# Q and K by Strassen's seven products on pairs of W tiles and token chunks

## The chip, the cores and the metric

One core of one Trainium2 chip. The time is that of one execution on the device in microseconds; a kernel's figure is the median of its runs. PE is the matrix engine, DVE, ACT and POOL are the vector, scalar and GpSimd engines, SP is the engine that issues most DMAs.

## The reference

A layer norm, an attention block of 32 heads and a Mish MLP on the same normalised input, joined by a gate (cut to what is computed; all fp32):

```python
B, S, D, H, F = 1, 2048, 1024, 32, 3584
xn = layernorm(x)                                    # no scale, no shift
q, k, v = split(xn @ wqkv)                           # wqkv: D x 3D, 32 heads of 32
p = softmax(q @ k.T * 32 ** -0.5)                    # per head
s = (p @ v) @ wo
h = xn @ w1 + b1
m = (h * tanh(softplus(h))) @ w2
out = x + s * silu(m)
```

## The kernel before

Every large product is made in three matmuls on numbers split into a high part, rounded to the format that PE takes at full pace, and a low part, the rest: high x high, high x low, low x high (THREE). ACT makes a high part by a copy, DVE or POOL the low part by a subtraction (`low`, L295). A matmul is 128 x 128 by 128 x 512.

The program has these stages, one behind the other on PE.

1. **V, two passes** (L473 to L559). The first pass takes x in 16 tiles of 128 tokens, normalises and transposes it into xc, four chunks of 512 tokens (chunk c has two tiles, xc[c][0] and xc[c][1], of four k slices each, high and low side by side), and makes V's first 512 columns from it. The second pass (L548) makes the other 512 columns. Each group v_group is 24 matmuls into one of 8 PSUM banks; ACT copies it out, SP stores it. Beside them w1_early (L449) loads tiles of w1, POOL splits them, and SP stores the split tiles to w1s for the MLP: 12 tiles (W1_V). x_store keeps chunks 1 to 3 in DRAM (xs).
2. **Q and K** (L682 to L713). 16 tiles of 128 columns (f even Q, odd K) times 4 chunks, 24 matmuls each (L688) into one of 8 banks. ACT copies the high part out, DVE makes the low part, ACT's queue stores both. qk_load and qk_split bring the next tile of W. Beside it presplit (L659) takes half tiles: the other 16 tiles of w1 and the first 16 row tiles of w2 (W2_Q), 64 jobs, each a load, a POOL cast, a POOL subtraction and a store. From f = 12 on, four score matmuls of head 0 (s_mm, L613) stand behind each group, with a row maximum each on DVE.
3. **Attention with the MLP** (L719 to L1273). PE's order comes from a planner, Plan: it keeps a clock for each engine and rings for buffers and banks, and at each step takes the instruction that is ready and has the least due time. Streams: t (scores transposed, exponentials on ACT), s (scores for the maxima of the next heads), h and y (first and second product of the MLP) and the narrow column matmuls pv (P times V) and zp. POOL adds up the exponentials z, 15 adds of 128 x 2048 a head (L874); seven p tiles hold exponentials (ring "p"). LEAN is a row of digits, one for each 21 us of the planner's PE clock, each choosing a set of small shifts of due times. Row tiles of w2 that were not split in stage 2 are split during the MLP's first chunk (w2_op, L963): SP loads half a tile, ACT makes the high part, POOL the low part (L987), SP stores it to w2s.
4. **Output projection** (op, L1215).

DMAs of SP and ACT go out in the order of their queues. Where an instruction waits, all behind it on the same engine wait too.

## Time and profile before

| what | value |
|---|---|
| median of 3 runs (lowest to highest) | 3391.5 us (3391.26 to 3392.14) |
| profiled execution, first to last instruction (span) | 3390.7 us |
| median of the runs less that span | 0.8 us |
| V, second pass, and Q and K | 110 to 201 us, 201 to 565 us |
| attention with MLP, output projection | 565 to 3212 us, 3212 to 3386 us |
| PE's granted clock, mean | 1.00 |

The page gives no time of the profiled execution beside its span. Rows of groups read: line, engine, operation, written tile <- read tiles, shapes, count, busy us, mean ns of one, idle time just before and what ended it. Rows of windows read: from and to in us, length, busy us (and count) of PE, of PE's weight loads, of DVE, ACT and POOL, the granted clock, the share of the DMA engines, GB/s. Rows of a timeline and of the chain begin with start and length in us. Rows of waits end with total us, times, longest us.

### The profile page before, as it was taken

The numbers are of one execution on the slowest core, as the hardware profiler recorded it, in microseconds if no ns is written. First come the engines' busy times: TensorE is split into PE (matmuls) and PEld (weight loads), VectorE is DVE, ScalarE is ACT, GpSimd is POOL, SyncE is SP. The second block draws the span as 40 slices with busy tenths as digits, with TensorE's granted clock in tenths as the row PEclk, the third lists the DMA queues.
The fourth block names the chain that finished last, engine by engine and source line by source line (L and its number), as shares of the span: only waits on it lengthen the run. The fifth ranks groups of instructions, "written<-read, shape, count | busy, mean of one in ns | idle before, by whom it ended". The sixth has DMA issues, their size and how long they took to land.

```text
span 3390.7 us, 45610 instructions
## 1 busy us (share of the span) xinstructions
PE 3375.7 (100%) x17059; PEld 2495.2 (74%) x17059; DVE 2350.2 (69%) x3765; ACT 1960.6 (58%) x3112; POOL 2432.7 (72%) x724
## 2 busy tenths in 40 slices
PE   8999999999999999999999999999999999999999
PEld 7888888677777777776777777777777767777787
DVE  6111136888887787887888778878888788886543
ACT  5211113666667767666666676666666666666621
POOL 1323334888899998888888888888888888888800
PEclk9999999999999999999999999999999999999999
DMA  6977878334344454343333544343445433333382
GB/s 204 303 263 266 286 262 265 106 113 125 100 131 135 137 172 150 104 121 107 119 113 113 168 131 120 105 128 106 122 116 189 118 118 113 113 119 119 131 308 83
DMA packets 284465, 517.02 MB, mean 152 GB/s; under 512 B 88186, under 2 KB 134266, under 8 KB 261498
## 3 DMA queue, kind: packets, MB, share of 16 engines
q1 hardware_dynamic: 264532, 472.42, 44.4%
q10 hardware_dynamic: 19712, 41.69, 3.3%
q8 instruction: 135, 2.21, 0.3%
q14 instruction: 86, 0.70, 0.1%
HBM read 374.31 MB, written 138.67 MB: 151 GB/s over the span
## 4 chain that ended last, share of the span: by engine, by line
PE 99%; DMA 0%; ACT 0%; DVE 0%; SPq 0%; issue 0%
PE y L1116 18%; PE h L1026 18%; PE t L845 14%; PE s L763 13%; PE pv L892 13%; PE qk L688 10%; PE v L357 5%; PE op L1215 5%; PE zp L918 1%; PE pt L426 0%; PE s L615 0%; DMA qstack<-mt 0%; DMA vraw<-in_A_wqkv_dram 0%; PE mtp L592 0%; ACT p L284 0%
## 5 line engine op out<-in xcount | busy, mean ns | idle before, releaser
L874 POOL TENSOR_TENSOR z<-z,p 128x2048 f32<-128x2048 f32 x448 | 2067.6, 4615 | 176.6 <-ACT p L284 149.2
L284 ACT ACTIVATE p<-t,zero 128x512 f32<-128x512 f32 x2048 | 1382.0, 689 | 601.8 <-PE t L845 588.9
L769 DVE TENSOR_REDUCE mx<-s 128x1 f32<-128x512 f32 x1984 | 1327.7, 686 | 402.2 <-PE s L763 398.1
L1116 PE MATMUL y<-w,act 128*128 128x512 f32 x2688 | 932.7, 390 | 0.1
L845 PE MATMUL t<-qstack,kstack 128*128 128x512 f32 x2048 | 798.2, 392 | 1.3 <-DMA qstack<-mt 1.3
L763 PE MATMUL s<-kstack,qstack 128*128 128x512 f32 x1984 | 774.8, 392 | 0.0
L1026 PE MATMUL h<-xr,w 128*128 128x512 f32 x2016 | 704.3, 390 | 0.0
L1116 PEld LDWEIGHTS y<-w,act 128*128 128x128 f32 x2688 | 503.6, 188 | 114.7 <-issue 5.9
L845 PEld LDWEIGHTS t<-qstack,kstack 128*128 128x128 f32 x2048 | 383.8, 188 | 109.4 <-issue 21.0
L892 PE MATMUL pv<-p,v 128*32 128x512 f32 x4096 | 459.3, 594 | 0.0
L763 PEld LDWEIGHTS s<-kstack,qstack 128*128 128x128 f32 x1984 | 370.9, 188 | 110.6 <-issue 18.4
L1026 PEld LDWEIGHTS h<-xr,w 128*128 128x128 f32 x2016 | 378.1, 188 | 83.4 <-issue 4.2
L688 PE MATMUL qk<-xc,qkw 128*128 128x512 f32 x1536 | 351.0, 389 | 0.0
L688 PEld LDWEIGHTS qk<-xc,qkw 128*128 128x128 f32 x1536 | 288.1, 188 | 59.8
L892 PEld LDWEIGHTS pv<-p,v 128*32 128x32 f32 x4096 | 123.4, 110 | 283.1 <-issue 282.0
L1138 DVE TENSOR_TENSOR yacc<-yacc,y 128x512 f32<-128x512 f32 x416 | 282.9, 681 | 44.1 <-PE y L1116 43.0
L874 POOL TENSOR_TENSOR z<-p,p 128x2048 f32<-128x2048 f32 x32 | 148.0, 4626 | 210.2 <-PE zp L918 108.7
L1026 PE MATMUL h<-xc,w 128*128 128x512 f32 x672 | 230.1, 391 | 0.1
L295 DVE TENSOR_TENSOR qst<-qk,qst 128x512 fp32r<-128x512 f32 x64 | 44.3, 692 | 258.1 <-ACT qst L287 250.3
L287 ACT ACTIVATE qst<-qk 128x512 fp32r<-128x512 f32 x64 | 38.3, 598 | 306.0 <-PE qk L688 280.0
L676 POOL CAST pw<-praw 128x512 fp32r<-128x512 f32 x64 | 40.1, 627 | 236.0 <-DMA w1s<-pw 124.5
L357 PE MATMUL v<-vw,xc 128*128 128x512 f32 x768 | 180.7, 394 | 0.0
(94 smaller groups left out, 2372.1 us busy)
## 6 DMA issues: line engine op xcount, KB each, us to landing
w<-w1s SPq DMA_DIRECT2D x112, 1024.0 KB, 5.1
w<-w2s SPq DMA_DIRECT2D x200, 512.0 KB, 4.8
qstack<-qs SPq DMA_DIRECT2D x96, 256.0 KB, 6.4
kstack<-ks SPq DMA_DIRECT2D x96, 256.0 KB, 5.9
praw<-in_B_w_dram SPq DMA_DIRECT2D x64, 256.0 KB, 4.9
qs<-qst ACTq DMA_DIRECT2D x32, 512.0 KB, 3.8
w1s<-pw SPq DMA_DIRECT2D x32, 512.0 KB, 5.0
ks<-qst ACTq DMA_DIRECT2D x32, 512.0 KB, 4.3
```

Of the source, the lines that this page charges most:

```text
L284: nc.scalar.activation(out_, in_, fn, bias=zero if bias is None else bias, scale=scale)
L357: nc.tensor.matmul(ps, xc[t // 4][k // HK][:, a, k % HK, (t % 4) * P:(t % 4 + 1) * P], vw[i, k // 2][:, b, k % 2], start=n == 0, stop=n == ...
L688: nc.tensor.matmul(ps, w[:, a, k], xc[c][k // HK][:, b, k % HK], start=n == 0, stop=n == 3 * KT - 1)
L763: nc.tensor.matmul(sp_, qst[h % 3][:, qt * P:(qt + 1) * P], kst[h % 3][:, kc * 512:(kc + 1) * 512], start=True, stop=True)
L769: nc.vector.reduce_max(tiles["mx"][:, qt, kc:kc + 1], tiles[qt, kc], axis=AX.X)
L845: nc.tensor.matmul(tp, kst[h % 3][:, kt * P:(kt + 1) * P], qst[h % 3][:, c * 512:(c + 1) * 512], start=True, stop=True)
L874: nc.gpsimd.tensor_tensor(zs[h], pts[T - 1] if kt == 1 else zs[h], pts[T], ALU.add)
L892: nc.tensor.matmul(pv[h][c * DH:(c + 1) * DH, :], vt[h][:, k, :], pts[T - kt + k][:, c * 512:(c + 1) * 512], start=k == 0, stop=k == NT - 1)
L1026: nc.tensor.matmul(t["h"], w1t[n][:, a, k], xts_[c][k // HK][:, b, k % HK], start=i == 0, stop=i == 3 * KT - 1)
L1116: nc.tensor.matmul(t["y"], acts[n][:, p, s * P:(s + 1) * P], w2t[m_][:, q], start=j == 0 and i == 0, stop=j == YB - 1 and i == 2)
L1138: nc.vector.tensor_tensor(ya, ya, t["y"], ALU.add)
L1215: nc.tensor.matmul(ps[t, dh], ohl[t // 4, k][:, a, s * P:(s + 1) * P], wt[k][:, b, r], start=k == 0 and i == 0, stop=k == KT - 1 and i == 2)
```

## The change

**Products.** Chunks go in pairs, (2, 3) and then (0, 1), and the Q tile and the K tile of the same number form a pair with the two halves of k. The 2 x 2 blocks (k half by Q or K; k half by chunk) are multiplied in seven products in place of eight (the form with S1 to S4 and T1 to T4). There are 16 pairs (q 0 to 15), each with 7 products of 12 matmuls. W's blocks A11, A12, A22 and the sums S1 to S4 are split into pieces of half a W tile, two to a tile, made two and three products ahead: ACT the high, DVE the low part. POOL makes the sums of W for the next q. A tile of W is loaded twice, once for each pair of chunks.

**Accumulators.** PSUM has two each of x, y, z and s. Products 0 and 2 go into x, 1, 3 and 5 into y, 4 and 6 into z, each later one added onto the earlier. Between them ACT (e0) or DVE (e1, e3) reads the bank; products 2, 4, 5 and 6 end in a chunk of Q or K.

**Sums of x.** In V's second pass, whose token tiles now go in the order of chunks 1, 3, 0, 2, `t_half` makes the four sums of x for both pairs on DVE, split by ACT and DVE. For (0, 1) all four go to DRAM (ts, staged in the ring of x tiles), for (2, 3) three stay in the place of chunk tiles that are done with, and one goes to DRAM. During q 7 five tiles are loaded over X's tiles for the second pair.

**Splits.** W1_V is 8 and W2_Q 0: 8 w1 tiles are split beside V, 20 beside Q and K (three half jobs a q, none in q 7 and 8), all 28 of w2 beside the MLP's first chunk. Two score matmuls of head 0 stand behind each product from q 11 on. LEAN has other digits, and the banks' order and the planner's start values at the border of stage 3 are changed.

```diff
-W1_V = 12
+W1_V = 8
-W2_Q = 16
+W2_Q = 0
...
-LEAN = ("83700575777567776073778780867478770777713777737708777777777777788"
+LEAN = ("13000510047567756073468724860620770704718277635355470747314774488"
...
+    def w_sum(eng, q, which, out_):
+        (r0, r1), done = raws[q], sums.setdefault(q, {})
+        done[which] = out_
+        a, b, how = {S1: lambda: (r1[:, :HK], r1[:, HK:], ALU.add), S2: lambda: (done[S1], r0[:, :HK], ALU.subtract),
+                     S3: lambda: (r0[:, :HK], r1[:, :HK], ALU.subtract),
+                     S4: lambda: (r0[:, HK:], done[S2], ALU.subtract)}[which]()
+        eng.tensor_tensor(out_, a, b, how)
+
+    def piece(n, eng):
+        q, i = divmod(n, 7)
+        if n % 2 == 0:
+            pieces["tile"] = w1_tile(f"wq{n // 2}")
+        w = pieces[n] = pieces["tile"][:, :, n % 2 * HK:n % 2 * HK + HK]
...
+        copy(w[:, 0], src, scale=-1.0 if i == A22 else 1.0)
+        if i == A22:
+            nc.vector.scalar_tensor_tensor(w[:, 1], src, -1.0, w[:, 0].bitcast(F32), op0=ALU.mult, op1=ALU.subtract)
+        else:
+            low(eng, w[:, 1], src, w[:, 0])
...
+    def t_half(p, k, half):
...
+        if half == 0:
+            whole(t[0], c0, 0)
+            whole(t[1], c1, 0)
+            less(t[0], t[1], t[0])
+            whole(t[2], c1, 1)
+            less(t[1], t[2], t[1])
+            split(0, t[0], None if p else xc[1][1])
+            split(2, t[1], None if p else xc[1][0])
+        else:
+            less(t[2], t[2], t[0])
+            whole(t[3], c0, 1)
+            less(t[3], t[2], t[3])
+            split(1, t[2], None if p else xc[3][0])
+            split(3 if p else 4, t[3], None)
+
+    for i, t in enumerate([4, 5, 6, 7, 12, 13, 14, 15, 0, 1, 2, 3, 8, 9, 10, 11]):
         v_group(1, t)()
...
+        t_half(1 if i < 8 else 0, i % 8 // 2, i % 2)
...
+    psq = psum(qb, "psq", 2)
...
+    BANK = ("x", "y", "x", "y", "z", "y", "z")
+    NEXT = {0: (X[1][1], ts[1]), 1: (X[1][3], ts[2]), 2: (X[1][4], ts[0]), 3: (X[1][5], ts[3]),
+            4: (X[1][6], xs[1][:, :, HK:])}
...
+            if i == 0:
+                copy(e[0], ps)
+            elif i in (1, 3):
+                plus(e[i], ps, e[0])
+            elif i == 2:
+                out_(q, 0, c0, ps)
+            elif i == 4:
+                plus(e[3], ps, e[3])
+                out_(q, 1, c1, e[3])
+            else:
+                plus(ps, ps, e[0] if i == 5 else e[1])
+                out_(q, 1 if i == 5 else 0, c0 if i == 5 else c1, ps)
...
-    for f in range(2 * KT):
-        for c in range(NC):
-            qk_group(f, c if f < 2 * KT - 1 else (c + 1) % NC)
-            presplit()
...
+    q_load(0, ring_of(0))
+    q_load(1, ring_of(1))
+    x_load(xr, ts[4])
+    sums[0] = {}
+    for which in (S1, S2, S4):
+        w_sum(nc.vector, 0, which, s_tile(which))
+    first_s = iter([(qt, kc) for qt in range(NT) for kc in range(4)])
+    for q in range(NQ):
+        bank_, e = {}, {}
+        for i in range(7):
+            n = 7 * q + i
+            after = product(q, i, bank_, e)
+            if n >= 2 and n % 2 == 0:
+                for m in (n + 2, n + 3):
+                    if m < 7 * NQ:
+                        piece(m, nc.vector)
+            later.tick()
+            if q >= 11:
+                for qt, kc in [x for _, x in zip(range(2), first_s)]:
+                    s_mm(0, qt, kc)
+            after()
+            if q == KT - 1 and i in NEXT:
+                x_load(*NEXT[i])
+            if i == 3:
...
+                if q + 2 < NQ:
+                    q_load(q + 2, ring_of(q + 2))
+            if q + 1 < NQ:
+                for which in {3: (S1, S2), 4: (S3,), 5: (S4,)}.get(i, ()):
+                    w_sum(nc.gpsimd, q + 1, which, s_tile(which))
+            if i in (0, 2, 5) and q not in (KT - 1, KT):
+                presplit()
```

How the order of instructions changes is shown at two places.

*The border of V and Q.* DVE before, from the first low parts of a Q tile (qkw) on; qst is a part of Q or K on its way out:

```order
L576 MEMSET kstack0_1786 32x2048
L577 MEMSET kstack0_1786 2x2048
L583 MEMSET hl_1793 128x128
L585 MEMSET pad2_1795 128x32
L295 TENSOR_TENSOR qst0_0_1825<-qk0_0_1800,qst0_0_1825 128x512
L295 TENSOR_TENSOR qkw1_1831<-qkraw1_1723,qkw1_1831 128x512 x2
L295 TENSOR_TENSOR qst0_1_1864<-qk0_1_1839,qst0_1_1864 128x512
L295 TENSOR_TENSOR qst0_2_1898<-qk0_2_1873,qst0_2_1898 128x512
L295 TENSOR_TENSOR qst0_3_1933<-qk0_3_1908,qst0_3_1933 128x512
```

DVE in the change (its own line numbers), from the last sum of x (ts0_3_4) on. ws4, ws1, ws6 are the sums S1, S2, S4 of q 0, e the sums in the accumulators, wq the pieces:

```order
L293 TENSOR_TENSOR ts0_3_4_1929<-turned_1259,ts0_3_4_1929 128x512
L548 TENSOR_TENSOR ws4_1957<-raw1_1940 128x512
L548 TENSOR_TENSOR ws1_1959<-ws4_1957,raw0_1939 128x512
L548 TENSOR_TENSOR ws6_1961<-raw0_1939,ws1_1959 128x512
L760 TENSOR_TENSOR e0_1_1994<-q0_y_1981,e0_0_1976 128x512
L293 TENSOR_TENSOR wq2_2008<-ws4_1957,wq2_2008 128x512
L560 SCALAR_TENSOR_TENSOR wq2_2008<-raw1_1940,wq2_2008 128x512
L293 TENSOR_TENSOR qst0_0_2_2013<-q0_x_1963,qst0_0_2_2013 128x512
L760 TENSOR_TENSOR e0_3_2034<-q0_y_1981,e0_0_1976 128x512
L293 TENSOR_TENSOR wq3_2055<-ws6_1961,wq3_2055 128x512
L293 TENSOR_TENSOR wq3_2055<-raw2_1941,wq3_2055 128x512
```

Before, memsets and then the first group's low part stood here; now three sums that need raw0 and raw1 stand ahead of e0_1, which reads the bank y of product 1.

SP before at the same place:

```order
L363 DMA vs1_79<-vst1_14_1725 128x512
L363 DMA vs1_79<-vst1_15_1753 128x512
L291 DMA zeros_151<-qstack0_1785 32x2048
L667 DMA praw1_12_0_1828<-in_B_w1_dram 128x4x128
L304 DMA qkraw2_1836<-in_A_wqkv_dram 128x8x128
L667 DMA praw1_12_1_1867<-in_B_w1_dram 128x4x128
L667 DMA praw1_13_0_1901<-in_B_w1_dram 128x4x128
L291 DMA w1s12_92<-pw1_12_0_1829 256x1x512
```

And in the change, from the last store of V on:

```order
L357 DMA vs1_79<-vst1_11_1896 128x512
L289 DMA ts4_140<-ts0_3_4_1929 256x1x512
L540 DMA raw0_1939<-in_A_wqkv_dram 128x8x128
L540 DMA raw1_1940<-in_A_wqkv_dram 128x8x128
L540 DMA raw2_1941<-in_A_wqkv_dram 128x8x128
L540 DMA raw3_1942<-in_A_wqkv_dram 128x8x128
L289 DMA xr_1938<-ts4_140 128x2x512 x4
L721 DMA praw8_0_1978<-in_B_w1_dram 128x4x128
```

Tiles of W for the first products stood ahead of V's last stores; now the load of raw0 and raw1 stands behind the store of the last sum of x (ts4), and xr is loaded from that sum.

*DVE with the scores of head 0.* Before, at the first group of f = 13 (mx is a maximum over one score matmul, nm and hl belong to the finished maxima):

```order
L295 TENSOR_TENSOR qst13_0_3790<-qk13_0_3765,qst13_0_3790 128x512
L295 TENSOR_TENSOR qkw14_3796<-qkraw14_3602,qkw14_3796 128x512 x2
L619 TENSOR_REDUCE mx0_4_3805<-s0_4_0_3803 128x1
L619 TENSOR_REDUCE mx0_4_3805<-s0_4_1_3807 128x1
L619 TENSOR_REDUCE mx0_4_3805<-s0_4_2_3810 128x1
L619 TENSOR_REDUCE mx0_4_3805<-s0_4_3_3813 128x1
L295 TENSOR_TENSOR hl_1793<-nm0_0_3758,hl_1793 128x4
L295 TENSOR_TENSOR qst13_1_3847<-qk13_1_3822,qst13_1_3847 128x512
```

In the change, q 12 from its product 3 to product 5:

```order
L760 TENSOR_TENSOR e12_3_4007<-q12_y_3926,e12_0_3921 128x512
L293 TENSOR_TENSOR wq45_4028<-ws6_3865,wq45_4028 128x512
L293 TENSOR_TENSOR wq45_4028<-spare_3290,wq45_4028 128x512
L677 TENSOR_REDUCE mx0_4_3944<-s0_5_2_4036 128x1
L677 TENSOR_REDUCE mx0_4_3944<-s0_5_3_4039 128x1
L760 TENSOR_TENSOR e12_3_4007<-q12_z_4015,e12_3_4007 128x512
L293 TENSOR_TENSOR qst12_1_1_4043<-e12_3_4007,qst12_1_1_4043 128x512
L677 TENSOR_REDUCE mx0_4_3944<-s0_6_0_4063 128x1
L677 TENSOR_REDUCE mx0_4_3944<-s0_6_1_4066 128x1
L760 TENSOR_TENSOR q12_y_3926<-q12_y_3926,e12_0_3921 128x512
L293 TENSOR_TENSOR qst12_1_0_4070<-q12_y_3926,qst12_1_0_4070 128x512
```

Before, four maxima stood with one low part (and in one group of four with two of a W tile) per 24 matmuls. Now two maxima stand per 12, and between them the pieces, the sums of the accumulators and, right behind such a sum, the low part of Q or K whose high part ACT copies from it.

192 lines of the change are left out of this document (115 added, 77 removed).

## The prediction

> **What bounds the kernel now.** I read the page's first and fourth parts, then the waits of PE, then the windows by stage.
>
> ```profile
> PE 3375.7 (100%) x17059; PEld 2495.2 (74%) x17059; DVE 2350.2 (69%) x3765; ACT 1960.6 (58%) x3112; POOL 2432.7 (72%) x724
> ...
> PE 99%; DMA 0%; ACT 0%; DVE 0%; SPq 0%; issue 0%
> ```
>
> The first row gives busy shares, the second the chain that ended last. A busy PE may still be waiting inside, so the waits must agree. These are all that PE has (total, times, longest):
>
> ```profile
> PE pt L426 <- ACT x L284: 9.1, 1, 9.1
> PE t L845 <- DMA qstack<-mt: 1.3, 2, 0.9
> ```
>
> One wait at the start and 1.3 us in all the rest. PE is the bound in every stage, and its instructions are the time. By stage (V's second pass, Q and K, attention with MLP):
>
> ```profile
> core 0: us, PE busy (x) PEld busy (x) DVE busy (x) ACT busy (x) POOL busy (x), PEclk, DMA share, GB/s
> ...
> 110.00:201.08 91.08, 91.08 (x403) 75.42 (x402) 5.09 (x8) 13.76 (x24) 34.02 (x36) 1.00 0.93 315
> 201.08:564.60 363.52, 363.52 (x1606) 300.86 (x1605) 104.26 (x165) 55.58 (x101) 122.54 (x128) 1.00 0.78 264
> ...
> 564.60:3212.20 2647.60, 2646.01 (x13792) 1891.08 (x13791) 2108.45 (x3320) 1796.35 (x2833) 2257.14 (x538) 1.00 0.41 126
> ```
>
> In Q and K PE is full, while DVE is busy 104 and POOL 123 of 364 us. There is room for the change's extra elementwise work. In V's second pass DMA is at 0.93, where there is little room. The clock is 1.00 throughout.
>
> **What goes.** Q and K lose 1536 - 16 x 7 x 12 = 192 matmuls.
>
> ```profile
> L688 PE MATMUL qk<-xc,qkw 128*128 128x512 f32 x1536 | 351.0, 389 | 0.0
> ...
> 201.08 266.56 PE qk L688 x1176
> 468.55 5.44 PE qk L688 x24
> 474.89 5.44 PE qk L688 x24
> ```
>
> 389 ns is one matmul with its fill and drain. The pace comes from the chain: 266.56 / 1176 = 0.2267 us, and again 5.44 / 24. From 468.55 to 474.89 are 6.34 us, which is 24 qk and 4 score matmuls of head 0 at that pace, without a gap. So 192 x 0.2267 = **43.5 us** leave the path, and a product of 12 takes 2.72 us. This is the most that can be gained: the attention part has the same matmuls as before, and PE's order shows 96 runs of narrow column matmuls (pv, zp) before and after, so switching costs the same.
>
> **What is added beside PE.** The durations of the same forms:
>
> ```profile
> L295 POOL TENSOR_TENSOR w1p<-w1e,w1p 128x512 fp32r<-128x512 f32 x24 | 31.0, 1291 | 1.9
> ...
> L295 DVE TENSOR_TENSOR qst<-qk,qst 128x512 fp32r<-128x512 f32 x64 | 44.3, 692 | 258.1 <-ACT qst L287 250.3 <-DMA w2s<-pw 4.7 <-DMA qstack<-qs 3.1
> ...
> L287 ACT ACTIVATE qst<-qk 128x512 fp32r<-128x512 f32 x64 | 38.3, 598 | 306.0 <-PE qk L688 280.0 <-DMA ks<-qst 15.4 <-DMA qstack<-qs 5.7
> L676 POOL CAST pw<-praw 128x512 fp32r<-128x512 f32 x64 | 40.1, 627 | 236.0 <-DMA w1s<-pw 124.5 <-DMA w2s<-pw 97.4 <-DMA praw<-in_B_w_dram 13.4
> ```
>
> In a row behind each other DVE's take less (timeline, start and length):
>
> ```profile
> 468.92 1.28 DVE L295 TENSOR_TENSOR qkw<-qkraw,qkw 128x512 fp32r<-128x512 f32 x2
> 470.12 2.48 DVE L619 TENSOR_REDUCE mx<-s 128x1 f32<-128x512 f32 x4
> ```
>
> That is 0.64 for a low part and 0.62 for a maximum. Five places decide what of the 43.5 is kept.
>
> *V's second pass.* DVE gets 12 instructions in two groups, 12 x 0.64 = 7.7 of 2 x 5.44 = 10.9 us, so it keeps up. DMA is tighter:
>
> ```profile
> 136.00:184.00 48.00, 48.00 (x214) 39.74 (x213) 0.00 (x0) 5.29 (x9) 20.71 (x23) 1.00 1.01 353
> ...
> xs<-xc SPq DMA_DIRECT2D x12, 1024.0 KB, 5.6
> w1s<-w1p SPq DMA_DIRECT2D x12, 1024.0 KB, 5.5
> vs<-vst SPq DMA_DIRECT2D x32, 256.0 KB, 2.5
> ```
>
> Full, DMA moves 353 GB/s. In the first eight groups the change issues 8 stores of V, 4 w1s stores, 3 loads of w1 (512 KB), 4 stores of x and 16 stores of sums (512 KB): 19,968 KB in 43.5 us, which takes 58. In the last eight it is 9,216 KB, 27 us: together 85 of 87 us. PE has 8 PSUM banks, so it can run 8 groups (43.5 us) ahead of a late ACT; a backlog of 14 us in the middle is covered if it is gone at the end. I take 0 here, and up to 8 if DVE's sums come late at the end. Below nothing it cannot go, since PE never waited there.
>
> *The border of V and Q.* All 8 banks are no cover here: each product uses one of three accumulators.
>
> ```profile
> 200.92 5.38 PE L688 MATMUL qk<-xc,qkw 128*128 128x512 f32 x23
> 201.17 0.60 ACT L287 ACTIVATE vst<-v 128x512 f32<-128x512 f32 x1 [4.84 <-PE v L357]
> ...
> 202.21 0.38 SPq L291 DMA_DIRECT2D zeros<-qstack  x1
> ...
> DMA to landing us min/median/max: 4.2/5.0/5.8
> ```
>
> The first two rows are today's border, the third is an issue on SP's queue; the last is the landing of qkraw, the same 512 KB in the same shape as raw0 and raw1. Counted from the first Q matmul: ACT starts at 0.25 and does the copy of V and two high parts by 2.1, DVE's last low part is done at 2.8. SP's store of it stands ahead of raw0 and raw1, at some 0.4 an issue raw1 goes out at 3.6 and lands at 8.6. DVE then makes three sums (1.9), and only behind them in its order e0_1: 8.6 + 1.9 + 0.7 = 11.2. Product 3 adds into the bank that e0_1 reads and could start at 3 x 2.72 = 8.2. **3 us** are lost; 2.2 with the shortest landing, up to 11 with DVE 8 us late.
>
> *Products of q 0 to 10.* DVE has 16 instructions x 0.64 = 10 of 7 x 2.72 = 19.0 us. An accumulator must be read within the next product: 2.72 less 0.25 and 0.69 leaves 1.8 us of slack. Ahead of that read stand at most two low parts (1.3). DMA has some 5.5 MB a q (two raw loads, three splits, four stores), 290 GB/s in place of 264, so its share of 0.78 becomes some 0.86. I take **1 us** with the memsets (two of 1.8 us on DVE) that move from the border into q 9. Bounds: 0, and the chain rival below.
>
> *From q 7 to 8.* Twenty loads of 256 KB, two raw loads and four stores are 8.4 MB in 19.0 us, 24 us at 353 GB/s; the first chunk is due 8 products (22 us) after its load. ACT's stores of Q and K wait behind them. **2 us**, between 0 and 5.
>
> *q 11 to 15, with two score matmuls of head 0 behind each product.* Per q PE has 98 x 0.2267 = 22.2 us. DVE has 14 maxima, 7 low parts of W, 5 sums and 4 low parts of Q and K: 30 x 0.64 = 19.2 us. Three of the last four low parts stand right behind the sum that ACT must copy first (0.60 and two hand-overs), with nothing between, so DVE idles some 0.75 each: 21.4. To that comes POOL, busy per q with four sums and three splits, 7 x 1.29 + 3 x 0.63 = 10.9 us, half the time:
>
> ```profile
> 403.49 1.29 POOL L295 TENSOR_TENSOR pw<-praw,pw 128x512 fp32r<-128x512 f32 x1
> ...
> 403.64 2.30 DVE L295 TENSOR_TENSOR qkw<-qkraw,qkw 128x512 fp32r<-128x512 f32 x2
> ...
> L295 DVE TENSOR_TENSOR qkw<-qkraw,qkw x32: 680/684/1697, 191.4 to 520.4; 128x512 fp32r<-128x512 f32 x32
> ...
> qstack<-qs SPq DMA_DIRECT2D x96, 256.0 KB, 6.4
> ```
>
> Two low parts that take 1.28 took 2.30 here, having started 0.15 us after POOL's instruction: 1.0 us of waiting for its end. The third row has the low parts' least, middle and longest, 1697 ns. With POOL busy half the time and a mean rest of 0.6, each of 8 low parts from SBUF waits 0.3: 2.4 more, 23.8 against 22.2. Over 32 products (4.6 q) that is 1.6 x 4.6 = 7 us, a little of it made up in the light products 0 to 3. **6 us**, between 0 and 20 (a whole 1.29 in half the cases: 8 x 0.65 = 5.2 in place of 2.4, 4.4 x 4.6). Head 0's six loads (last row) are issued some 11 us before q 11 needs them and take 6.4; I count them as covered, up to 3 if SP is late.
>
> The Trainium skill, SBUF — State Buffer, section Who interferes with whom, speaks against this change: a VectorE instruction with two SBUF inputs and a GpSimd instruction that reads SBUF exclude each other for the whole instruction. The row above agrees, with 1.0 us of waiting. Without the rule q 11 to 15 would need 21.4 of 22.2 us and lose nothing (3355); by the rule with its waits at the mean they lose the 6 (3361).
>
> *MLP's first chunk.* POOL gets 32 more low parts of W2, x 1.29 = 41 us, spread over the first chunk:
>
> ```profile
> L295 POOL TENSOR_TENSOR w<-w2r,w 128x512 fp32r<-128x512 f32 x24 | 31.0, 1290 | 1.2 <-ACT w L287 1.2
> ...
> 1040.00:1120.00 80.00, 80.00 (x418) 56.17 (x417) 65.03 (x107) 56.84 (x93) 74.54 (x23) 1.00 0.47 148
> 1120.00:1200.00 80.00, 80.00 (x420) 56.85 (x419) 59.98 (x96) 55.90 (x90) 74.37 (x23) 1.00 0.44 133
> 1200.00:1280.00 80.00, 79.93 (x420) 56.60 (x420) 67.58 (x109) 53.61 (x86) 74.65 (x22) 1.00 0.60 190
> ```
>
> Today's 24 fall into these windows: 16 adds of z and 6 or 7 low parts in 80 us, POOL 93% busy, PE full. The change holds the same density (56 in some 656 us, 6.8 in 80) for longer. What hides them is the seven p tiles; without that cover each would cost its 1.29. **1 us**, between 0 and 41. On ACT they are 32 x 0.63, with 24 us free in 80.
>
> **The sum.** Against the profiled execution: 3390.7 - 43.5 + 3 + 1 + 2 + 6 + 1 = 3360.2. The median of the runs is 0.8 above the span: **3361.0**.
>
> **Rivals.** (a) *All of it is kept:* DVE's order has slack everywhere and the raw tiles land early. For it: 30% use in Q and K. Against: the border's order of SP and DVE. 3391.5 - 43.5 = 3348, to 3352. Chance 0.10.
> (b) *DVE and POOL exclude each other and DVE becomes the bound* in q 11 to 15 and late at V's end: 20 instead of 6, and 11 instead of 3: 3361 + 22 = 3383. For it the 2.30 us row; against it that the middle of today's low parts is 684 ns with POOL busy a third of the stage. Chance 0.16, from 3372 to 3384. The Trainium skill's section named above is this rule.
> (c) *The chain through one accumulator becomes the pace of all 112 products, and the kernel is slower.* Matmul, DVE's sum or ACT's copy, matmul again into the same bank: the slack is 1.8 us, and ACT's queue also holds the stores of Q and K, which wait for DVE's low part and for a free transfer; a store late by more than that stops the copies behind it. It decides from 43.5 / 112 = 0.39 us a product; at 0.6 it costs 67 us, 3415. For it: ACT waited for a store of Q or K (15.4 us in the qst row above); against: those were few. Chance 0.10, 0.03 of it within 0.2%.
> (d) *POOL becomes the bound in the first chunk:* the 41 us come back, 3402. Against it the three windows. Chance 0.04.
>
> **How the numbers follow.** The forecast, 3352 to 3372, has 0.60. With all of (b) and most of (a) 3349 to 3385 hold 0.83; left out are (c), (d) and the end of (a). Faster by over 0.2% (below 3384.7; about what a measurement of this kernel can tell from no change) are the forecast, (a) and (b): 0.86. Within 0.2%: 0.04. Slower: 0.10.
>
> **What would show it.** 1344 matmuls on the line of the products at 0.2267. A gap of PE of about 3 us before the fourth product of q 0, waiting for DVE; gaps under 1 us in q 11 to 15, waiting for DVE's maxima; the attention part as long as before (some 2648 us) with POOL at 93% from the start. Wrong it would be with gaps between all products, or with PE waiting for exponentials or p tiles in the first 650 us of attention.

## The result, and the profile after

The change is slower by a little, where the prediction had it 30 us faster. The median of 11 runs is 3398.74 us (3395.07 to 3401.17), that of the kernel before beside it 3391.88; the ratio is 1.0017, with a 95% interval of 1.0008 to 1.0025. The profiled execution has a span of 3398.2 us against 3390.7.

The page's first and fourth parts of the changed kernel, the busy shares and the chain:

```profile
PE 3355.3 (99%) x16867; PEld 2461.8 (72%) x16867; DVE 2540.1 (75%) x4020; ACT 2037.3 (60%) x3272; POOL 2516.8 (74%) x759
...
PE 91%; DMA 3%; DVE 3%; POOL 1%; ACT 1%; issue 1%; SPq 1%; ACTq 0%; POOLq 0%; DVEq 0%
```

PE has 192 matmuls less, and 3355.3 us of busy time in place of 3375.7. But the chain, 99% PE before, now goes through DMA, DVE and others for 9% of the span. The windows of the changed kernel by stage (V's second pass, Q and K, attention with the MLP) say where:

```profile
110.00:200.81 90.81, 90.81 (x403) 75.18 (x402) 60.65 (x90) 30.23 (x54) 24.74 (x24) 1.00 0.95 338
200.81:562.82 362.01, 338.51 (x1414) 270.60 (x1413) 246.15 (x341) 110.11 (x199) 177.60 (x144) 0.96 0.87 278
562.82:3218.95 2656.13, 2651.36 (x13791) 1888.57 (x13790) 2100.40 (x3317) 1801.91 (x2866) 2295.62 (x570) 1.00 0.42 129
```

V ends when it did. Q and K take 362.0 us against 363.5: 43.5 us of matmuls are gone and only 1.5 us of time. PE stands idle there for 23.5 us, and its clock is 0.96 in the mean. The attention part takes 2656.1 us against 2647.6. With 0.1 us less at the start and 0.6 more at the end, these are the 7.5 us between the spans. The longest waits of PE after the start:

```profile
PE q_y L771 <- DVE e L760: 5.2, 2, 5.0
PE q_y L771 <- ACT xc L285: 4.8, 1, 4.8
PE q_z L771 <- DMA xc<-xs: 4.1, 3, 3.5
PE q_y L771 <- DMA xc<-ts: 3.0, 3, 1.3
PE q_z L771 <- DVE e L760: 2.0, 1, 2.0
PE s L887 <- DVE mx L893: 1.5, 3, 0.7
```

For the table below I took, from the starts of all matmuls, the time from the first matmul of a product to that of the next, less 0.2267 us for each matmul of 512 columns between them. What is left is *lost* time: waits, slow clock and all.

| lost in (us) | the change | predicted |
|---|---|---|
| q 0 and 1 (border of V and Q) | 18.2 | 3 |
| q 2 to 7 | 0.0 | 1 (q 0 to 10) |
| q 8 and 9 | 17.6 | 2 |
| q 10 to 15 | 6.3 | 6 |
| attention, longer than before | 8.5 | 1 |

**The border.** PE's timeline of the changed kernel (start, length, and in brackets the wait ahead): product 1 in two pieces, products 2, 3 and 4.

```profile
210.48 0.49 PE L771 MATMUL q_y<-xc,wq 128*128 128x512 f32 x1 [4.75 <-ACT xc L285]
...
212.76 5.28 PE L771 MATMUL q_x<-xc,wq 128*128 128x512 f32 x12
223.07 5.34 PE L771 MATMUL q_y<-xc,wq 128*128 128x512 f32 x12 [5.02 <-DVE e L760]
228.25 2.92 PE L771 MATMUL q_z<-xc,wq 128*128 128x512 f32 x12
```

The predicted gap ahead of product 3 is there, with the predicted releaser, but it is not the only one, and products 2 and 3 take 5.3 us in place of 2.9. DVE and then SP of the changed kernel at the same place:

```profile
199.25 1.36 DVE L293 TENSOR_TENSOR xc<-turned,xc 128x512 fp32r<-128x512 f32 x1 [5.29 <-ACT xc L285]
...
202.24 3.48 DVE L575 TENSOR_TENSOR turned<-xc 128x512 f32<-128x512 f32 x2
...
211.84 0.69 DVE L293 TENSOR_TENSOR ts<-turned,ts 128x512 fp32r<-128x512 f32 x1
220.27 0.69 DVE L548 TENSOR_TENSOR ws<-raw 128x512 f32<-128x512 f32 x1 [7.73 <-DMA raw<-in_A_wqkv_dram]
```

```profile
212.56 0.52 SPq L289 DMA_DIRECT2D ts<-ts  x1
213.17 5.09 SPq L540 DMA_DIRECT2D raw<-in_A_wqkv_dram  x4
```

The last low part of x's sums ends 11.7 us after Q's first matmul, where the prediction had 2.8; the store, the load of raw0 and raw1 and DVE's three sums follow from it as it said. On its way DVE stood 5.3 us for ACT (first row): in ACT's order the copies of q 0's pieces stood ahead, and these waited for W's raw tiles, of which the second took some 11 us to come. Two sums then took 3.48 us beside low parts on POOL, 1.29 without them.

**q 8 and 9.** PE's timeline of the changed kernel in products 5 and 6 of q 8, then a window over the time from the first load of a tile of X to product 6, then the loads' row in the list of DMA issues:

```profile
387.85 0.98 PE L771 MATMUL q_y<-xc,wq 128*128 128x512 f32 x3 [1.29 <-DMA xc<-ts]
390.08 0.96 PE L771 MATMUL q_y<-xc,wq 128*128 128x512 f32 x3 [1.25 <-DMA xc<-ts]
...
396.21 2.90 PE L771 MATMUL q_z<-xc,wq 128*128 128x512 f32 x6 [3.48 <-DMA xc<-xs]
```

```profile
353.00:396.00 43.00, 36.42 (x154) 28.13 (x152) 17.92 (x29) 11.91 (x21) 6.15 (x5) 0.95 1.00 340
```

```profile
xc<-ts SPq DMA_DIRECT2D x16, 512.0 KB
```

A k slice of a tile is 512 KB. The prediction counted 256. The twenty loads are 10.5 MB, and the DMA engines are full for 43 us. In q 9 it is DVE that is late (its timeline in the changed kernel; e is the sum that releases the bank of product 6):

```profile
417.64 1.76 DVE L645 MEMSET kstack<- 32x2048 f32 x1 [0.48 <-issue]
419.89 1.76 DVE L646 MEMSET kstack<- 2x2048 f32 x1 [0.49 <-DVE kstack L645]
...
421.85 0.65 DVE L760 TENSOR_TENSOR e<-q_z,e 128x512 f32<-128x512 f32 x1
```

**The clock.** Windows of the changed kernel with PEclk as the third number from the right:

```profile
211.10:217.80 6.70, 6.05 (x14) 4.46 (x14) 1.28 (x2) 1.11 (x2) 0.00 (x0) 0.50 0.60 167
...
392.00:405.50 13.50, 9.42 (x21) 5.80 (x20) 7.70 (x9) 3.53 (x6) 5.80 (x4) 0.50 1.05 333
422.70:426.00 3.30, 3.30 (x8) 2.63 (x9) 2.80 (x3) 1.51 (x3) 2.79 (x3) 0.50 0.78 269
```

After each of the longer waits PE is granted half its clock, and a matmul takes 5.28 / 12 = 0.44 us. Part of this falls into time that would have been waited anyway. What stands behind the last wait of each loss does not: 2.5 us at product 3 of q 0, 2.1 from the last late tile of q 8 on, 1.7 at product 6 of q 9, by the starts of the matmuls 6.3 us in all. The prediction had no such term.

### The profile page after: what moved, and what is told of

It reads as the page before. It is cut to its first block, busy times and chain, and to the rows that moved or that the text cites. A ratio compares the mean times of both kernels' runs of the same rounds, so it can differ in the third digit from the quotient of the medians.

```text
span 3398.2 us, 45889 instructions
## 1 busy us (share of the span) xinstructions
PE 3355.3 (99%) x16867; PEld 2461.8 (72%) x16867; DVE 2540.1 (75%) x4020; ACT 2037.3 (60%) x3272; POOL 2516.8 (74%) x759
## 4 chain that ended last, share of the span: by engine, by line
PE 91%; DMA 3%; DVE 3%; POOL 1%; ACT 1%; issue 1%; SPq 1%; ACTq 0%; POOLq 0%; DVEq 0%
PE y L1240 18%; PE h L1150 18%; PE t L969 14%; PE s L887 13%; PE pv L1016 13%; PE op L1339 5%; PE v L351 3%; PE q_y L771 2%; PE q_x L771 2%; PE q_z L771 2%; PE zp L1042 1%; DMA w1e<-in_B_w_dram 1%; PE pt L420 0%; DMA praw<-in_B_w_dram 0%; DVE mx L677 0%
## 5 line engine op out<-in xcount | busy, mean ns | idle before, releaser
L887 PEld LDWEIGHTS s<-kstack,qstack 128*128 128x128 f32 x1984 | 369.9, 188 | 121.7 <-issue 23.5
L351 PEld LDWEIGHTS v<-vw,xc 128*128 128x128 f32 x768 | 143.4, 189 | 30.3 <-ACT xc L285 0.6
L1150 PEld LDWEIGHTS h<-xc,w 128*128 128x128 f32 x672 | 125.9, 188 | 26.6 <-ACT p L282 0.7
L771 PE MATMUL q_y<-xc,wq 128*128 128x512 f32 x480 | 120.5, 399 | 13.8 <-DVE e L760 5.2
L285 ACT ACTIVATE act<-h 128x512 fp32r<-128x512 f32 x112 | 66.6, 595 | 88.9 <-DVE h L1199 87.9
L771 PEld LDWEIGHTS q_y<-xc,wq 128*128 128x128 f32 x480 | 91.1, 192 | 36.7 <-DVE e L760 5.7
```

Of the source, the lines that this page charges most:

```text
L351: nc.tensor.matmul(ps, xc[t // 4][k // HK][:, a, k % HK, (t % 4) * P:(t % 4 + 1) * P], vw[i, k // 2][:, b, k % 2], start=n == 0, stop=n == ...
L771: nc.tensor.matmul(ps, w[:, a, k], xx[:, b, k], start=n == 0 and i in (0, 1, 4), stop=n == 3 * HK - 1, skip_group_check=i not in (0, 1, 4))
L887: nc.tensor.matmul(sp_, qst[h % 3][:, qt * P:(qt + 1) * P], kst[h % 3][:, kc * 512:(kc + 1) * 512], start=True, stop=True)
L1150: nc.tensor.matmul(t["h"], w1t[n][:, a, k], xts_[c][k // HK][:, b, k % HK], start=i == 0, stop=i == 3 * KT - 1)
```

## The experiments

The theory after the traces: three separate losses, at the border from DMA in V's second pass, at q 8 from DMA after q 7, in attention from POOL's splits of W2, the first two made longer by the clock. Two programs below share q 0 to 9 with the change word for word (no split of W1 from q 11 on, and W2's low parts cut short). They lost 18.5 and 18.6 us in q 0 and 1, 14.4 and 16.4 in q 8 and 9; single profiles differ by that much. In the tables "lost" is worked out as above.

### The attention part alone

```diff
-W2_Q = 16
+W2_Q = 0
-LEAN = ("83700575...")
+LEAN = ("13000510...")
```

(The digits are shortened here; Q and K stay those of the kernel before.)

> The kernel before with only the change's third stage: W2_Q 0 and the change's LEAN; Q and K stay as before. My theory, that the 8.3 us which the attention part became longer come from POOL having all 28 tiles of W2 to split beside the MLP's first chunk: the attention part is again 6 to 9 us longer than before (2654 to 2657 us in place of 2647.6), and the time is 3397 to 3400. Rival, that they come from the other state in which the new Q and K leave banks, queues and DMA at the border: 2647 to 2650, time 3390 to 3393.

Measured: 3424.06 us, ratio 1.0093 (1.0078 to 1.0108); the attention part took 2678.9 us. Neither theory: 31 us longer. The planner's start values (which bank is free when) were still those of before, so that it wrote another order, and for that order the digits were never chosen. So the run was repeated with the change's start values:

```diff
-    for i in (7, 3, 4, 6, 0, 2, 5, 1):
+    for i in (0, 1, 2, 6, 3, 7, 4, 5):
-    plan.rings["b"] = [(t, i) for i, t in enumerate((0.0, 0.2, 0.3, 0.9, 1.5, 2.1, 2.7))]
-    plan.at["DVE"] = 2.8
+    plan.rings["b"] = [(t, i) for i, t in enumerate((0.0, 0.0, 0.0, 0.0, 0.0, 0.0, 0.3))]
+    plan.at["DVE"] = 2.5
```

> The kernel before with W2_Q 0, the change's LEAN and, unlike the run on the attention part alone, the change's start values of the planner (order and times of the banks, DVE's clock) too, so that the order of the third stage is the change's own, row for row. In that run the attention part took 2678.9 us. Theory, that LEAN's digits fit one order only and that the rest of the change's loss there is POOL's load: the attention part takes 2653 to 2659 us and the time is 3396 to 3402. Rival, that POOL's 28 tiles cost the 31 us whatever the order, and the change escapes them through its own Q and K: 2670 or more, time above 3412.

Measured: 3403.79 us, ratio 1.0031 (1.0020 to 1.0043), attention 2655.2 us. With the change's order behind the old Q and K the part is as long as in the change (2656.1), 7.6 us over before. So the loss belongs to the third stage's own order and load, not to Q and K. The total is 1.8 us above the range: the banks did not come free as these start values say, and attention began 4.9 us after the last Q matmul, not 1.6.

### POOL's low parts of W2 cut short

```diff
-            low(nc.gpsimd, w2t[m][:, 1], w2r[m], w2t[m][:, 0])
+            if f < 12:
+                low(nc.gpsimd, w2t[m][:, 1], w2r[m], w2t[m][:, 0])
+            else:
+                nc.gpsimd.memset(w2t[m][:, 1].bitcast(F32), 0.0)
```

> The change; for 16 of the 28 row tiles of W2 POOL fills the low part with zeros in place of the subtraction (so W2's low part is left out there), with the order of all engines as it was. By POOL's memset in the change's trace (1.81 us for 2048 columns) such a fill is some 0.45 us in place of 1.29, in 32 instructions some 27 us of POOL less. Theory, that the attention part is longer because POOL, 94% busy beside the MLP's first chunk, gives the p tiles back late, and scores for the next heads run ahead until DVE's maxima stop PE (4.3 us between 1200 and 1300 us): what is lost there falls below 1.5 us, and the attention part from 2656 to 2650 to 2653. Rival, that the order with its digits makes it, whatever POOL does: 2655 to 2657, with the loss at 1230 us as before. Time 3392 to 3396 or 3398.

Measured: 3401.01 us, ratio 1.0024 (1.0015 to 1.0033); attention 2656.1 us, what the change took to 0.1 us. Rows of this run's groups, and its waits of PE in the attention part:

```profile
L1115 POOL MEMSET w<- 128x512 f32 x32 | 16.9, 527 | 0.0
...
PE s L887 <- DVE mx L893: 1.6, 3, 0.7
```

POOL had 32 x (1.29 - 0.53) = 24 us less to do, and nothing came back: between 1200 and 1300 us the change lost 4.4 us, this run 4.6 and the kernel before 1.0. (The total is 3.0 us above the range that I gave; these were lost in Q and K.) My theory falls: POOL being busy is not what costs the time. What remains is the order that the planner wrote, together with what else the third stage has more to do. At 1230 us PE's timeline of the changed kernel is

```profile
1230.66 0.51 PE L887 MATMUL s<-kstack,qstack 128*128 128x512 f32 x1 [0.25 <-DVE mx L893]
1231.86 0.49 PE L887 MATMUL s<-kstack,qstack 128*128 128x512 f32 x1 [0.69 <-DVE mx L893]
...
1234.25 1.10 PE L887 MATMUL s<-kstack,qstack 128*128 128x512 f32 x2 [0.59 <-DVE mx L893]
```

with no t matmul from 1227.5 to 1247.4. From the starts of all t matmuls up to 1500 us: the longest stretch without one is 19.8 us in the change, 19.8 in the run with the same plan and 12.3 before. Where t is missing, PE gets scores whose maxima DVE cannot make so fast. This place accounts for 3.4 of the 8.5 us; the other 5 lie spread over the part in small lots, and no run names their cause. The planner counts W2's splits on POOL's clock when it writes the order; whether that or the digits lengthened the stretches, or the 32 further copies on ACT and transfers in that part cost something of their own, was not tried.

### Matmuls of no use in the waits

```diff
+    FILL = {(0, 1, 3): 20, (0, 3, 0): 20, (8, 5, 1): 5, (8, 5, 2): 5, (8, 6, 0): 15, (9, 6, 0): 8}
...
         for k in range(HK):
+            warm(FILL.get((q, i, k), 0))
```

> The change, with matmuls of no use (their results are never read) put into the waits of PE seen in its trace: 20 ahead of the last k slice of product 1 of q 0, 20 ahead of product 3, 5, 5 and 15 around the late tiles of q 8, 8 ahead of product 6 of q 9. Each lot is shorter than the wait in which it stands, so that it should not delay what follows. Theory, that the clock halves after such a wait and the matmuls behind it then take 0.44 us in place of 0.2267: no rows at half clock remain in Q and K, product 3 of q 0 and those around q 8 to 9 run at 0.2267, and the time falls by 5 to 9 us (3390 to 3394). Rival, that the slow matmuls behind a wait are slow for another reason (late data, the port): the time stays within 1 us, or grows by what of the lots does not fit.

Measured: 3401.04 us, ratio 1.0023 (1.0013 to 1.0033): no gain. With the added matmuls counted as lost, 19.4 us went in q 0 and 1 and 17.8 in q 8 and 9 (the profile is of the longest of ten executions, 3405.99 us). This run's PE at the border (warm are the added ones):

```profile
213.60 3.01 PE L780 MATMUL q_x<-xc,wq 128*128 128x512 f32 x12
216.44 4.69 PE L768 MATMUL warm<-xc 128*128 128x512 f32 x20
224.20 4.61 PE L780 MATMUL q_y<-xc,wq 128*128 128x512 f32 x12 [3.06 <-DVE e L760]
```

Product 2 now runs at full pace (3.01 in place of 5.28), so the slow matmuls were the clock. But product 3 still waits for data that come at their own time (223.1 in the change, 224.2 here): what the clock had cost product 2 was time that would have been waited anyway. The added matmuls ended 3.06 us before these data came, and product 3 still took 4.61. So the run shows that slow matmuls ahead of a later wait cost nothing; what half clock costs behind the last wait it took away in q 9 alone (product 6: 3.01 in place of 4.58). Of the 5 to 9 us that I expected in the time nothing came.

### W1 beside V's first pass

```diff
-W1_V = 8
+W1_V = 5
...
-        if t % 3 == 2 and t > 2:
+        if t % 2 == 0 and t > 2:
             w1_early()
...
-        if i % 2 == 0 and i < 10:
-            w1_early()
...
-            if i in (0, 2, 5) and q not in (KT - 1, KT):
+            if i in (0, 2, 5) and q not in (KT - 1, KT) or i == 4 and 0 < q < 5:
                 presplit()
```

> The change, with the split of W1 tiles taken out of V's second pass: five tiles are split beside the first pass, at every second group, and the other 23 beside Q and K (a fourth half tile in q 1 to 4). Theory, that the loss of 18.2 us in q 0 and 1 comes from the DMA engines being full in V's second pass, with ACT and DVE waiting in the x ring behind the loads of W1, so that the sums of x end late: DVE's last sum of x moves from 211.8 us to below 204, the loss in q 0 and 1 falls to 4 to 8 us, time 3385 to 3389. Rival, that it comes from the order at the border itself (raw tiles of W behind the last sum's store, two low parts of POOL on the shared port): loss above 14, time above 3394.

Measured: 3393.85 us, ratio 1.0004 (0.9995 to 1.0014), 4.9 us less than the change; lost in q 0 and 1 10.5, between theory and rival. The same window of V's second pass in the change and then in this run:

```profile
160.00:180.00 20.00, 20.00 (x90) 16.56 (x89) 14.07 (x24) 6.52 (x11) 3.75 (x4) 1.00 1.04 411
```

```profile
160.00:180.00 20.00, 20.00 (x90) 16.57 (x89) 14.17 (x23) 5.49 (x11) 0.08 (x1) 1.00 0.71 233
```

DVE's timeline of this run at its end:

```profile
204.28 0.69 DVE L293 TENSOR_TENSOR ts<-turned,ts 128x512 fp32r<-128x512 f32 x1
212.77 0.69 DVE L548 TENSOR_TENSOR ws<-raw 128x512 f32<-128x512 f32 x1 [7.80 <-DMA raw<-in_A_wqkv_dram]
```

The last sum moved from 211.8 to 204.3, and the wait for an xc tile in product 1 is gone. So W1's share of V's second pass (8 MB of transfers issued there, and the places in the x ring that wait for them) made nearly half of the loss. The rest stands, by this trace, behind the load of raw0 and raw1. Q and K take 9.8 us less than in the change, the attention part 2.8 more.

### The late blocks of q 0 kept

```diff
+    keep = pool(ph, "keep", 1)
...
+            a22 = kept(S2)
+            nc.sync.dma_start(a22, wqkv[HK * P:, D:D + P].rearrange("(k p) f -> p k f", p=P))
...
-            w_sum(nc.gpsimd, 0, S1, s12[:, 0])
+            w_sum(nc.gpsimd, 0, S1, kept(S1))
...
+            w_sum(nc.gpsimd, 0, S4, kept(S4))
...
-    q_load(0, ring_of(0))
     q_load(1, ring_of(1))
     x_load(xr, ts[4])
-    sums[0] = {}
-    for which in (S1, S2, S4):
-        w_sum(nc.vector, 0, which, s_tile(which))
```

> The run with W1 split only beside V's first pass, in which 10.5 us were still lost in q 0 and 1, with one more edit: the sums S1 and S4 and the block A22 of q 0 are made or loaded in V's second pass, into a pool that lives on, so that raw0 and raw1 are not loaded again behind the store of the last sum of x and DVE has no sums of W ahead of e0_1. Theory, that the rest of the border's loss is that load (issued 205.6, landed 212.7 us): the loss in q 0 and 1 falls to 0 to 3 us, time 3384 to 3388. Rival, that product 5 then waits as long for xr, the last sum of x on its way through DRAM: the loss stays above 6, time above 3390.

Measured: 3395.40 us, ratio 1.0007 (0.9998 to 1.0016); lost in q 0 and 1 10.0. Product 3 no longer waits, but product 5 does (this run's PE; the last sum still ends at 206.4 us):

```profile
216.22 0.94 PE L777 MATMUL q_y<-xr,wq 128*128 128x512 f32 x3 [1.50 <-ACT qst L285]
218.40 0.97 PE L777 MATMUL q_y<-xr,wq 128*128 128x512 f32 x3 [1.24 <-DMA xr<-ts]
220.90 1.65 PE L777 MATMUL q_y<-xr,wq 128*128 128x512 f32 x3 [1.54 <-DMA xr<-ts]
```

The rival holds: behind the load of raw stood another wait for the same late sum, which goes to DRAM and back as xr.

### The sums of x ahead of ACT's copies of V

```diff
-        v_group(1, t)()
+        waiting.append(v_group(1, t))
+        if i > 2:
+            waiting.pop(0)()
...
-        if i in (12, 13):
-            for n in (2 * (i - 12), 2 * (i - 12) + 1):
+        if i in (14, 15):
+            for n in (2 * (i - 14), 2 * (i - 14) + 1):
...
+    for evac in waiting:
+        evac()
```

> The run at the border (W1 beside V's first pass, q 0's late blocks kept), in which 8.6 us were still lost in q 0, waiting for xr, with one more edit: ACT's copies of V's second pass are issued three groups later, behind the sums of x, and the pieces of q 0 two steps later, so that the sums of x no longer end at V's pace. Theory, that what is left of the border's loss is the last sum of x, which ACT's copy of V's groups holds back to V's end and which then goes to DRAM and back into xr: the last sum ends some 10 us earlier, and the loss in q 0 and 1 falls from 10 to 0 to 2 us; time 3385 to 3389. Rival, that the two DMAs in a row (store, load) or the two engines' shared port make it: loss above 6, time above 3392.

Measured: 3389.29 us, ratio 0.9990 (0.9981 to 0.9999); lost in q 0 and 1 4.2 us, of which 0.5 in q 0: nearly all that the theory takes for q 0, with 2 us more in q 1 than it allows. DVE's timeline of this run, the last sum of x and e0_1 of q 0:

```profile
187.42 0.69 DVE L293 TENSOR_TENSOR ts<-turned,ts 128x512 fp32r<-128x512 f32 x1
205.94 0.69 DVE L771 TENSOR_TENSOR e<-q_y,e 128x512 f32<-128x512 f32 x1 [17.83 <-PE q_y L782]
```

The last sum ends 24 us earlier than in the change. The cause of the border's loss is the time of that last sum: first DMA (W1, stores), then ACT's copies of V's groups, which stood ahead of the sums' copies and wait for PE (the pieces of q 0, which this run also moves back, were not tried by themselves). In q 1 3.8 us remain, waiting for pieces and e0 on ACT.

### The tiles of X first

```diff
-            move(zeros, qst[i][96:P, :])
-            nc.vector.memset(kst[i][96:P, :].bitcast(F32), 0.0)
-            nc.vector.memset(kst[i][96:98, :].bitcast(F32), 1.0)
+            later.at(3, lambda: move(zeros, qst[i][96:P, :]))
+            nc.gpsimd.memset(kst[i][96:P, :].bitcast(F32), 0.0)
+            nc.gpsimd.memset(kst[i][96:98, :].bitcast(F32), 1.0)
...
-                if q + 2 < NQ:
-                    q_load(q + 2, ring_of(q + 2))
+            if i == (5 if q == KT - 1 else 3) and q + 2 < NQ:
+                q_load(q + 2, ring_of(q + 2))
...
-            if i in (0, 2, 5) and q not in (KT - 1, KT):
+            if i in (0, 2, 5) and q not in (KT - 2, KT - 1, KT) or i == 4 and 0 < q < 4:
                 presplit()
```

> The change, with the five tiles of X alone on the DMA engines at q 7: no split of W1 in q 6 (they move to q 1 to 3), the W load of q 9 behind them instead of between them; and in q 9 the memsets of the stack tiles on POOL in place of DVE, the store of the zeros three products later. Theory, that the 17.6 us of q 8 and 9 come from 20 loads of 512 KB that are queued with other transfers, and from two memsets ahead of DVE's sum: the loss in q 8 falls from 12.4 to 3 to 7 us, that in q 9 from 5.2 to below 1.5, time 3386 to 3390. Rival, that the 10.5 MB of the tiles alone are too much in the time from their release to their use: the loss in q 8 stays above 9, time above 3393.

Measured: 3397.47 us, ratio 1.0014 (1.0005 to 1.0024). Lost in q 8 14.1 us, no better than the 12.4 of the change; in q 9 0.0 in place of 5.2. A window of this run from the first load on, and its product 6:

```profile
354.60:396.00 41.40, 35.80 (x153) 28.04 (x151) 16.17 (x25) 10.65 (x19) 5.13 (x4) 0.99 1.01 347
```

```profile
401.12 4.99 PE L771 MATMUL q_z<-xc,wq 128*128 128x512 f32 x12 [8.10 <-DVE e L760]
```

The rival holds for q 8: in this order too, 10.5 MB of tiles, 3.5 MB of Q and K and W's next raw tiles keep the engines full for 41 us. The raw tiles that went to the end of the queue are now the late ones; DVE stands behind them in its order. The theory holds for q 9: without the two memsets ahead of DVE's sum nothing is lost there. But not all of the 5.2 us was waiting for them. With the memsets still on DVE, three other runs (no split of W1 from q 11 on, the late blocks kept, the sums ahead of ACT's copies) lost 1.8 to 1.9 us in q 9: their waits of 1.6 us left the clock at full speed. In the change the wait was 2.0 us; 1.7 us of half clock followed it, and 1.3 were left over from q 8's waits.

### Two products of q 7 made within q 6

```diff
+    SEQ = [(q, i) for q in range(NQ) for i in range(7)]
+    for i, at in ((0, 1), (2, 4)):
+        SEQ.remove((KT - 1, i))
+        SEQ.insert(7 * (KT - 2) + at, (KT - 1, i))
...
+        for n, (q, i) in enumerate(SEQ):
```

> The run with X's tiles first, with one more edit: products 0 and 2 of q 7 are made within q 6 (behind its products 0 and 2), so that two of the five tiles can be loaded some 16 us earlier. In that run 14.1 us were lost in q 8, with the DMA engines full from 360 us on. Theory, that the loss there is the time which 10.5 MB of tiles and 3.7 MB of Q and K take after the first release, and no matter of order: the loss in q 8 falls by 8 to 12 us, to 2 to 6, time 3384 to 3389. Rival, that the loads just wait longer in SP's queue behind other transfers: loss in q 8 above 9, time above 3392.

Measured: 3390.56 us, ratio 0.9994 (0.9984 to 1.0003), 8.2 us less than the change and 1.6 above the expected range. Lost in q 8 2.4 us, in q 7 to 9 together 5.1. The longest wait of PE at this place, product 6 of q 8 in this run (issue: the profile shows no releaser):

```profile
390.77 3.00 PE L775 MATMUL q_z<-xc,wq 128*128 128x512 f32 x12 [2.10 <-issue]
```

The theory holds: it is the bytes between the first release and the first use, and with two of five tiles loaded some 16 us earlier most of the loss is gone.

### No split of W1 from q 11 on

```diff
-        move(w1t[n], w1s[n % FT])
+        move(w1t[n], w1s[n % FT % 21])
...
-    jobs = iter([(f, half) for f in range(W1_V, FT) for half in range(2)])
+    jobs = iter([(f, half) for f in range(W1_V, 21) for half in range(2)])
```

> The change, with the split of W1 left out from q 11 on (7 of the 28 tiles of W1 are never split, and the MLP reads other tiles in their place). POOL then has only the four sums of W in each q there. Theory, that the 6.3 us lost in q 11 to 15 come from low parts on DVE that wait for POOL's instructions to end: the loss there falls to 1 to 3 us. Rival, that DVE's own order (maxima, sums and low parts with their hand-overs to ACT) makes it: 5 to 6.5 us as before. The time falls by what is gained there, 0 to 5 us, and no more.

Measured: 3397.52 us, ratio 1.0013 (1.0004 to 1.0023); lost in q 10 to 15 7.2 us. Windows over q 11 to 15, of the change and of this run:

```profile
440.00:560.00 120.00, 117.49 (x505) 93.73 (x504) 99.83 (x153) 34.85 (x66) 53.68 (x46) 1.00 0.78 249
```

```profile
440.00:560.00 120.00, 116.68 (x501) 94.46 (x500) 93.33 (x152) 34.82 (x66) 21.84 (x16) 0.99 0.49 159
```

POOL's busy time falls from 53.7 to 21.8 us, DVE's from 99.8 to 93.3, and PE gains nothing. So DVE's busy time did hold some 6 us of waiting for POOL, as the prediction had it, but little of it on PE's path. The largest wait is that of the first score matmul behind head 0's loads (1.3 us lost there in the change, 4.1 in this run's first two products, 1.5 to 4.8 over q 11 in the profiles of all variants of the change, so that this part varies by itself). Behind it, in q 12 to 15, 3.1 us are lost in place of 4.8, in places of 0.4 to 1.0 us, the maxima's way over ACT and PE (mt) among them; the other variants lost 3.8 to 5.8 there. At most some 2 us of the 6.3 can be POOL's. The size of the prediction's term was right by luck, its cause wrong in the main.

### All that helped, together

The edits at the border (W1_V is 5) and at q 7 to 9 in one kernel, with load_head(0) three products earlier (beside the diffs above):

```diff
-            if i in (0, 2, 5) and q not in (KT - 1, KT):
+            if i in (0, 2, 5) and q not in (KT - 2, KT - 1, KT) or i == 4 and (q < 5 or q in (KT + 2, KT + 3)):
                 presplit()
-            if i == 3 and q == 10:
+            if i == 0 and q == 10:
                 load_head(0)
```

> All edits that took a loss away, in one kernel: W1 beside V's first pass, q 0's late blocks kept, the sums of x ahead of ACT's copies of V, the two early products of q 7, the tiles of X alone in the queue, the memsets on POOL; and head 0's tiles loaded three products earlier. If the losses are separate and each is what I take it for: 0 to 2 us in q 0 and 1, 3 to 5 in q 7 to 9, 4 to 6 in q 11 to 15, the attention part 2655 to 2659 as in all runs of the change; the time is 3365 to 3373, faster than both kernels. If they have one common source, full DMA engines, then the transfers moved from one place come back at another: 3380 to 3388.

Measured: 3385.70 us, ratio 0.9978 (0.9969 to 0.9988). Lost: 4.4 in q 0 and 1, 1.9 in q 2 to 6, 7.4 in q 7 to 9, 10.1 in q 10 to 15; attention 2659.8. The losses of the single runs add up to some 17, here they are 23.8: part of what was moved comes back elsewhere, as the rival had it, and the time lies in the rival's range. Then with W1's eight early tiles all in V's first pass:

```diff
-W1_V = 5
+W1_V = 8
...
-        if t % 2 == 0 and t > 2:
+        if t in (4, 5, 6, 7, 8, 9, 10, 12, 14, 16):
             w1_early()
...
-            if i in (0, 2, 5) and q not in (KT - 2, KT - 1, KT) or i == 4 and (q < 5 or q in (KT + 2, KT + 3)):
+            if i in (0, 2, 5) and q not in (KT - 2, KT - 1, KT) or (q, i) == (0, 4):
                 presplit()
```

> The combined kernel, with all eight early tiles of W1 split beside V's first pass, where the DMA engines are busy 35 to 78% from 20 to 80 us (a step behind nearly every group), so that Q and K have 40 half tiles of W1 to split in place of 46, 4.5 MB less. In the combined kernel 23.8 us were lost in Q and K: 4.4 in q 0 and 1, 1.9 in q 2 to 5, 7.4 in q 7 to 9, 10.1 in q 11 to 15. Theory, that what is left in q 1 to 5 and about half in q 8 and 11 is full DMA engines: Q and K lose 15 to 20 us, the time falls by 4 to 9 us, to 3377 to 3382. Rival, that x's loads now wait for places in the ring behind W1's: the first pass and with it Q's start (200.8 us) come later by 2 us or more, and the time stays at 3384 to 3390.

Measured: 3382.73 us (3380.70 to 3385.78), ratio 0.9970 (0.9959 to 0.9981), the fastest kernel here, 0.7 us above the theory's range. Lost in Q and K 18.8 us (5.2, 0.0, 6.0, 7.6 in the four parts). The window of this run over Q and K:

```profile
201.40:540.60 339.20, 327.73 (x1414) 264.82 (x1412) 231.78 (x323) 107.99 (x195) 175.87 (x143) 0.99 0.91 285
```

Q and K take 339.2 us in place of 362.0, but only 16 of those 23 us arrive in the time: attention is 2662.9. Its first wait in this run, and SP's queue ahead of it:

```profile
PE t L979 <- DMA qstack<-mt: 5.0, 2, 4.1
```

```profile
539.77 5.49 SPq L289 DMA_DIRECT2D w<-w1s  x1
545.35 1.34 SPq L289 DMA_DIRECT2D qstack<-mt  x2
```

Scores of head 0's last quarter wait for their maxima, which go out behind a load that waits for a place; before, this wait was 1.3 us.

## Why the prediction was wrong

By its own steps:

- **192 matmuls, 43.5 us, leave the path: right.** Q 2 to 7 lose nothing in the change: 12 matmuls of 0.2267 us a product, no chain through an accumulator. Rival (c) is refuted.
- **"V's second pass: I take 0 here, and up to 8 if DVE's sums come late at the end": the step that failed first.** The count of 85 us of transfers in 87 was there, and I let a backlog of 14 us count as covered because PE has 8 banks. PE was covered. The sums were not: their transfers and W's raw tiles use the same DMA engines, the last sum ended 8.9 us later than I put it, and everything at the border hangs on it. The runs show it: 18.2 us lost with that sum ending at 212.5 us, 10.5 at 205.0, 10.0 at 206.4 with the reload of raw0 and raw1 gone, 4.2 at 188.1. The bound of 11 at the border was too low as well (18.2): products 1, 3 and 5 each hang on that sum by another way.
- **"Twenty loads of 256 KB ... 8.4 MB ... 2 us": a wrong factor.** They are 512 KB each, 13.6 MB in all and 39 us at the 353 GB/s that I used, in 19 us of products. From the release of the first tile to product 6 of q 8 there are 12 products, 32.6 us, so with the right factor the step would have given some 6 us before landing and clock; 12.4 were lost in q 8. The memsets, counted into 1 us in the prediction, cost q 9 some 2 of its 5.2; the rest was half clock.
- **No term for the clock.** The text said 1.00 throughout; that holds only while PE does not wait. Behind the last waits half clock cost some 2 us at each of three places, 6.3 in all, of 36 us lost in q 0, 1, 8 and 9. It is a missing term, but the waits come first, and with it the prediction would still have been some 30 us too low.
- **q 11 to 15, 6 us: 6.3 measured, luck in the main.** Without POOL's splits the time of these q does not fall, and at most some 2 us in q 12 to 15 can be put down to them. The rule that the prediction weighed (DVE and POOL exclude each other; the Trainium skill, SBUF — State Buffer, section Who interferes with whom) agrees with the trace where the two meet: two sums took 3.48 us beside POOL's low parts, 1.29 alone. That row lies at the border, on the way to the last sum; in q 11 to 15 it set little or nothing of the path.
- **First chunk of the MLP, 1 us: 8.5 measured.** The prediction took the third stage's order as equal because the counts of matmuls and of column runs were equal. The run with the same plan shows that the 8 us are in that stage, the run with the short fill that they do not come from POOL's busy time (rival (d) is refuted as a mechanism), and the run with digits of one order on another shows how much is in an order: 31 us. What in the order or in the further copies and transfers makes the 8 us stays open.

## What to carry to other kernels

Where DMA is as full as in V's second pass here (0.95), count the bytes of every tile from its shape, and ask who else than PE is behind them: a backlog that the matrix engine does not feel may still be late for the elementwise work that the next stage starts with. When a wait is removed and the next one ends at the same time, look for the one late thing behind both; here it was the last sum of x. A hand-tuned order belongs to its start conditions: equal counts of matmuls did not make equal times.

## What the runs showed of the hardware

- The same 512 KB load of a tile of W landed in 5.0 us (median) before, in 6.5 in the run with W1 beside the first pass, and in some 11 us (issued at 183.4; POOL, which waited for it, began at 194.9) in the change's V, where the engines were full.
- Full, the DMA engines moved 340 and 347 GB/s over 40 us of mixed loads and stores, but 411 in 20 us of V's second pass, nearly all stores. The Trainium skill (DMA: Bandwidth & Descriptors, Specifications) has some 358 GB/s of HBM for a core and 435 for the fabric; the mixed stretches lie below the first figure, the stores above it and below the second.
- PE's clock halved after 4.75 us of waiting, but also after 2.0 us (422.70 to 426.00 at 0.50), and stayed half for 3.4, 6.8 or 13.7 us. The Trainium skill (TensorE: Matmul & The Clock Gate, Part 1) gives a free-running window of some 3.4 us; the lengths agree, and the 2.0 us show that a wait shorter than a window can be enough. Waits of 2.10 and 2.51 us in the run with two early products left the clock at 1.00.
